# Start-up of a filter-and-mixer kernel: inputs of the first batch ahead of all else on two queues, more buffers for the token weights, second weights seven tiles ahead

## The chip, the cores and the metric

One core of one Trainium2 chip. The metric is the time of one execution in device microseconds (us), as the median of a kernel's runs. All runs told of here are of the fast state, at a granted TensorE clock of 0.988 to 0.995. Each ratio below is the mean time of one kernel's fast runs over that of the other's fast runs of the same rounds, so it is not quite the ratio of the medians that are quoted.

## The reference

A global filter along the sequence (transform, product with a complex filter, transform back), then an MLP mixer over tokens and over channels. Batch 8, sequence 3008, width 256, token width 256, channel width 1536.

```python
X = np.fft.rfft(x, axis=1)
Y = X * (filt_r + 1j * filt_i)[None]
x = np.fft.irfft(Y, n=3008, axis=1).astype(np.float32)
xt = x.transpose(0, 2, 1)
h = np.maximum(xt @ w_tok1, 0.0) @ w_tok2
u = x + h.transpose(0, 2, 1)
h2 = np.maximum(u @ w_ch1, 0.0) @ w_ch2
out = u + h2
```

All weights come as 64-bit floats and have to be converted on the chip.

## The kernel before

The start-up runs the filter of batch 0 alone, with nothing of the mixer to hide behind. Its x is multiplied by a first table (`wa0`), copied by ScalarE (ACT), turned by 16 VectorE (DVE) transposes, and then goes through 32 filter steps. A step takes a table `wb` (one load per two steps) and a piece of the filter `filt` (some loads per two steps), and its result is stored to memory as `g_tmp`, to be read back by token (`t4_load`). The token weights are loaded as raw words `st` and converted among the steps: one ACT and four DVE instructions, then either two TensorE (PE) additions and an ACT copy (`on_chip`) or one more DVE addition (`rounded`). One conversion goes through `begin` (issue its load), `copy` (first ACT instruction) and `end`.

```python
BY_PE = 6        # second token weights that PE adds up; the rest are rounded on DVE
EARLY = 12
# raw words of the weights, in buffers borrowed from later stages
early = [(up, "u")] * 2 + [(tp, "t")] * 2 + [(vp, "v")] * 2
late = [(t2p, "t2"), (t3p, "t3")]
stages = [(t4p, "t4")] * (A // 2) + early * 3 + late * 5      # A // 2 = 12

def filt_load(c, first):                    # first batch: everything on Pool's queue
    q = nc.gpsimd if first else nc.sync
    ...
def convert():                              # one tile: finish, start the next two's steps
    ended[0] += 1
    ...
    advance(end); advance(copy); advance(begin)

def x_load(b, c):                           # two loads a piece, all on SyncE
    where, tag = ((xp, "x"), (tp, "t"), (vp, "v"))[c % 3] if b == 0 else (xp, "x")
    ...
def w_load(c):                              # one table and one set of filter loads
    wbs[g] = wbp.tile([P, WC, P + KR], FP32, tag="wb", name="wb")
    nc.sync.dma_start(wbs[g], ...)
    filt_load(c, first)
...
# the driver: i < NXC (12) are the x steps, then 33 filter steps
    if i < NXC:
        if i in (0, 2, 4, 6): advance(begin)
        if i == 5: advance(copy)
        if i in (7, 9, 11): convert()
    else:
        if (i - NXC) % 3 == 2: convert()
        k = i - NXC - 2
        if 19 <= k < 25: t4_load(0, k - 19, 0, PARTS[1])   # read g_tmp back, on SyncE
        elif k == 25: next(second)                         # x of the next batch, on SyncE
        elif k in (30, 31): ...                            # more of g_tmp
...
for i in range(rounds, A // 2 + TC * N2 // NG):
    convert()
    ...
    if i == A // 2 + BY_PE - 1:
        sum_up()
        acc = token_sums(0)
h1s[0] = token_relu(acc)
```

Every store of `g_tmp` is issued by ACT.

Of the kernel before, what the change touches and what calls it, by code (L numbers as in the profile page):

```python
# [20 lines left out]
N2 = 64  # L21
# [3 lines left out]
K2 = 32  # L25
A = 24
KR = 4 * A
HALF = 64
XC = 2
NXC = A // XC  # L30
TC4 = 4
FB = 3
XB = 2
KC = 2
WC = 2
DT = 256
TC = DT // P
# [6 lines left out]
MT = 6  # L44
NG = 8
PARTS = (0, 64, 112)
BY_PE = 6
EARLY = 12
GROUPS = ((0,), (1, 2), (3, 4), (5, 6), (7,))


# [73 lines left out]
def kernel(  # L125
# [11 lines left out]
    nc = tc.nc  # L137
# [70 lines left out]
    def filt_load(c, first):  # L208
        t, k0 = filts[c % FB], c * KC

        q = nc.gpsimd if first else nc.sync
        for src, i, p0 in ((filt_r, 0, 0), (filt_i, 1, HALF)) + (() if first else ((filt_r, 0, HALF),)):
            q.dma_start(t[p0:p0 + A, i], raw(src, k0, [[64 * D, A], [D, KC], [1, D]]))
            lo = p0 + 32
            if k0 == 0:
                q.dma_start(t[lo:lo + A, i, 0, :], raw(src, 32, [[64 * D, A], [1, D]]))
            k = max(k0, 1)

            for j0, n in ((0, 16), (16, A - 1 - 16)):
                q.dma_start(t[lo + j0:lo + j0 + n, i, k - k0:KC, :],  # L220
                            raw(src, 64 * (j0 + 1) - k, [[64 * D, n], [-D, k0 + KC - k], [1, D]]))

    def filt_double(c):
# [2 lines left out]



    early = [(up, "u")] * 2 + [(tp, "t")] * 2 + [(vp, "v")] * 2
    late = [(t2p, "t2"), (t3p, "t3")]  # L230
    stages = [(t4p, "t4")] * (A // 2) + early * 3 + late * 5

    def stage(n):
        where, tag = stages.pop(0)
# [56 lines left out]
    def w1_load(i):  # L291
        st = stage(512)
        rows = moe_w_tok1.rearrange("(n2 n1) t -> n2 n1 t", n1=N1)
        q = nc.sync if i < EARLY else nc.gpsimd
        last = 2 * i + 2 == A
        if last:
            nc.gpsimd.memset(st.bitcast(U32)[HALF:P, 512:1024], 0)
        for h in range(2):
            n = 1 if last and h else 2
            lo = h * A + 2 * i  # L300
            q.dma_start(st[h * HALF:(h + 1) * HALF, 0:n * DT].rearrange("p (a t) -> p a t", t=DT),
                        rows[:, lo:lo + n, :])
        yield

        h = halves(st, 512, spare_pair())
        yield next(h)
        on_chip(wai_t, *next(h), 512, [(lambda v: v, w1[:, 2 * i:2 * i + 2, :].rearrange("p a t -> p (a t)"))])

    def w2_load(i):

        t, g = divmod(i, N2 // NG)
        n = NG * N1

        more = g + 1 < N2 // NG
        st = stage(512)
        nc.gpsimd.dma_start(st[:, 0:n + more], moe_w_tok2[ts(t, P), ds(g * n, n + more)])
        yield
        dst = w2[:, t].rearrange("p (a h n2) -> p h n2 a", h=2, n2=HALF)[:, :, ds(g * NG, NG), :]

        def some(h, nh, w):  # L320
            return (lambda v: bass.AP(tensor=v.tensor, offset=v.offset + h * A, ap=[v.ap[0], [A, nh], [N1, NG], [1, w]]),
                    dst[:, h:h + nh, :, 0:w])

        parts = [some(0, 2, A)] if more else [some(0, 1, A), some(1, 1, A - 1)]
        if i < BY_PE:
            h = halves(st, n + more, spare_pair())
            yield next(h)
            on_chip(ident, *next(h), n + more, parts)
        else:
            yield from rounded(st, n + more, parts, False)  # L330
# [44 lines left out]
    def advance(it):  # L375
        s = next(it, None)
        if s:
            next(s, None)

    def sum_up():  # L380
        while behind:
            behind.pop(0)[1]()

    def convert():

        ended[0] += 1
        while behind and behind[0][0] < ended[0] - 2:
            behind.pop(0)[1]()
        advance(end)
        advance(copy)  # L390
        advance(begin)



# [2 lines left out]
    def x_load(b, c):  # L397
        last = c == NXC - 1

        where, tag = ((xp, "x"), (tp, "t"), (vp, "v"))[c % 3] if b == 0 else (xp, "x")  # L400
        t = where.tile([P, XC, D], FP32, tag=tag, name="x")
        rows = x[b].rearrange("(n2 n1) d -> n2 n1 d", n1=N1)
        for h in range(2):
            n = XC - 1 if last and h else XC
            lo = h * A + c * XC
            nc.sync.dma_start(t[h * HALF:(h + 1) * HALF, 0:n, :], rows[:, lo:lo + n, :])
            if n < XC:

                nc.sync.dma_start(t[h * HALF:(h + 1) * HALF, n:XC, :], rows[:, lo:lo + 1, :])
        xs[b, c] = t  # L410

    def rows_of(t_d, b):
# [12 lines left out]
    def dft(bs):  # L425
# [9 lines left out]
                nc.sync.dma_start(wbs[g], (wbi0_d if first else wbi_d)[:, ts(g, WC), :])  # L435
            filt_load(c, first)

        ahead = 3 * XB if first else XB
        for u in todo[0:ahead]:
            x_load(*u)  # L440
        if not first:
            yield True
        for i, u in enumerate(todo):
            if first and i in (5, 8):
                w_load(i // 6)
            a_unit(*u)
            if i + ahead < len(todo):
                x_load(*todo[i + ahead])
            yield i + 1 < len(todo)
# [65 lines left out]
        for k in range(K2 + 1):  # L515
            if k < K2:
                b_unit(k)
                if k % KC == 0 and k // KC + 2 < K2 // KC:
                    t2_load(k // KC + 2)
                    w_load(k // KC + 2)  # L520
                if first and k % KC == KC - 1 and k + 1 < K2:
                    filt_double(k // KC + 1)
            if k >= 1:
                bi_unit(k - 1)
            yield
# [18 lines left out]
    def token_relu(acc):  # L544
        h1 = h1p.tile([P, TC, D], FP32, tag="h1", name="h1")
        nc.scalar.activation(out=h1, in_=acc, func=AF.Relu)
        return h1
# [219 lines left out]
    with tc.manual_schedule():  # L767
        nc.sync.dma_start(wa0, wa0_d)
        nc.vector.memset(turned[:, A:K2, :], 0.0)
        for t in filts:  # L770
            nc.vector.memset(t, 0.0)
        rounds = 0
        second = dft(GROUPS[1])
        for i, _ in enumerate(dft(GROUPS[0])):
            if i == 0:
                for t, src in ((wai_t, wait_d), (wa, wa_d), (wai, wai_d), (ident, ident_d)):
                    nc.scalar.dma_start(t, src)

            if i < NXC:
                if i in (0, 2, 4, 6):  # L780
                    advance(begin)
                if i == 5:
                    advance(copy)
                if i in (7, 9, 11):
                    convert()
                    rounds += 1
            else:
                if (i - NXC) % 3 == 2:
                    convert()
                    rounds += 1  # L790

                k = i - NXC - 2
                if 19 <= k < 25:
                    t4_load(0, k - 19, 0, PARTS[1])
                elif k == 25:
                    next(second)
                elif k in (30, 31):
                    for c in range(3):
                        t4_load(0, 3 * (k - 30) + c, PARTS[1], PARTS[2])
        for c in range(A // TC4):  # L800
            t4_load(0, c, PARTS[2], P)
        sum_up()
        both = wcp.tile([P, 2, JP, 7, P], FP32, tag="wc", name="wc")

        chan.extend((both[:, 0], both[:, 1]))
        for i in range(rounds, A // 2 + TC * N2 // NG):
            convert()
            if i - rounds < XB:
                next(second)
            if i == A // 2 + BY_PE - 1:  # L810
                sum_up()
                acc = token_sums(0)
        h1s[0] = token_relu(acc)
        for dh in range(DH):
            convert()
            u_part(0, 0, dh)
        for f in v_steps(0, 0):
            f()
        for _ in range(XB):
            next(second)  # L820
        group, todo, done = -1, iter(()), True

        def next_ready(b):
            return done or b != GROUPS[group][-1]

        for b, i, place in mix(next_ready):
            if group + 1 < len(GROUPS) and b == GROUPS[group + 1][0]:
                if not done:
                    raise AssertionError("the filter's steps don't fit beside the mixer's")
                group += 1  # L830
                done = group + 1 == len(GROUPS)
                todo = iter(()) if done else dft(GROUPS[group + 1]) if group else second
                spread = True

            if not done and (place == 1 or group == 0 and (spread and (place == 2 or i > 3) or place == 2 and i % 2)):
                spread = next(todo, "end")
                done = spread == "end"
# [30 lines left out]
```

## Time and profile before

2588.3 us in the median of three runs (2585.92 to 2592.76). The start-up falls into stages, whose joints stand in the timeline; what is left after the last conversion is the mixer.

| stage | from, to | before (us) |
|---|---|---|
| A | start to the first transpose | 31.14 |
| B | first transpose to the end of the last filter product | 91.01 |
| C | to the first sum `v` | 44.25 |
| D | to the end of the last channel-weight conversion | 56.22 |
| rest | to the end | 2364.6 |

B is 18.38 us (16 transposes and a hand-over, the same in every kernel below) and 72.63 us of filter steps; below, "B" is the second part alone.

### The profile page before, as it was taken

What the parts mean: (1) busy time and instruction counts of PE and PEld (TensorE: products, weight loads), DVE (VectorE), ACT (ScalarE), POOL (GpSimd) and SP (SyncE); (2) the same over time, 40 slices, a digit from 0 to 9 for tenths busy, and PEclk for the clock granted to TensorE, in tenths of its full rate; (3) what the DMA queues carried; (4) which work ended last, traced back from release to release, by engine and by line L of the source; (5) the groups of instructions that cost most, each with busy time, mean ns of one, the idle gap of its engine ahead of it and who ended that gap; (6) DMA issues with size and microseconds to landing.
All of it is one profiled execution on the core that took longest, in us unless ns stands there. A gap on an engine that the chain in (4) does not pass through costs nothing.

```text
span 2587.2 us, 31459 instructions
## 1 busy us (share of the span) xinstructions
PE 2505.6 (97%) x10952; PEld 2000.9 (77%) x10952; DVE 1816.0 (70%) x3458; ACT 691.2 (27%) x1347; POOL 526.9 (20%) x966
## 2 busy tenths in 40 slices
PE   5989999999999999999999999999999999999998
PEld 2556666788878777888787777788888888888887
DVE  6897888556675888746666788846678577647676
ACT  2433222123221222222321222212222122212222
POOL 3652211111211112112112111121121121211212
PEclk7999999999999999999999999999999999999999
DMA  6964333312232332202232233211232121100001
GB/s 167 232 195 155 109 106 103 106 48 90 90 90 64 88 88 71 80 17 89 90 96 77 75 84 87 80 31 57 90 85 75 50 64 53 25 9 8 17 12 21
DMA packets 151834, 205.20 MB, mean 79 GB/s; under 512 B 34216, under 2 KB 102034, under 8 KB 151676
## 3 DMA queue, kind: packets, MB, share of 16 engines
q1 hardware_dynamic: 81068, 115.65, 15.7%
q0 software_dynamic: 30656, 39.93, 6.4%
q10 hardware_dynamic: 39952, 47.61, 5.7%
q8 instruction: 87, 1.43, 0.2%
q14 instruction: 71, 0.58, 0.1%
HBM read 131.23 MB, written 71.83 MB: 78 GB/s over the span
## 4 chain that ended last, share of the span: by engine, by line
PE 78%; DVE 13%; issue 3%; DMA 3%; ACT 2%; SPq 0%; ACTq 0%; POOL 0%; DVEq 0%; POOLq 0%
PE ps_po L631 26%; PE ps_pg L597 15%; PE ps_pg L613 11%; PE ps_b L540 4%; PE ps_b L557 4%; DVE t L575 3%; DVE hh L575 3%; PE ps_acc L540 2%; PE ps_acc L557 2%; PE ps_acc L494 2%; PE ps_b L562 2%; PE ps_acc L417 2%; DVE u L575 2%; DVE s L575 1%; PE ps_b L470 1%
## 5 line engine op out<-in xcount | busy, mean ns | idle before, releaser
L575 DVE TENSOR_TENSOR hh<-ps_pg,s 128x512 f32<-128x512 f32 (+3 forms) x864 | 482.4, 586 | 624.4 <-ACT s L600 623.8
L676 POOL DMA_DIRECT2D out_dram<-r x757 | 409.8, 550 | 1949.1 <-ACT hh L618 929.0
L618 ACT ACTIVATE hh<-hh 128x512 f32<-128x512 f32 (+1 forms) x576 | 348.0, 621 | 1122.8 <-DVE hh L575 1122.8
L631 PE MATMUL ps_po<-t,wc 128*128 128x256 f32 (+1 forms) x2304 | 535.5, 375 | 5.4 <-DVE t L575 4.6
L631 PEld LDWEIGHTS ps_po<-t,wc 128*128 128x128 f32 x2304 | 434.5, 190 | 132.9 <-issue 53.3
L631 PE MATMUL ps_po<-hh,wc 128*128 128x256 f32 (+1 forms) x1728 | 413.2, 375 | 3.1 <-POOL wc L339 2.8
L597 PE MATMUL ps_pg<-v,wc 128*128 128x256 f32 (+1 forms) x1728 | 413.3, 375 | 0.2
L631 PEld LDWEIGHTS ps_po<-hh,wc 128*128 128x128 f32 x1728 | 327.5, 190 | 42.4 <-POOL wc L339 3.6
L597 PEld LDWEIGHTS ps_pg<-v,wc 128*128 128x128 f32 x1728 | 326.9, 190 | 40.5 <-DVE v L575 3.0
L613 PE MATMUL ps_pg<-u,wc 128*128 128x256 f32 (+1 forms) x1152 | 294.5, 378 | 7.0 <-DVE hh L575 6.5
L575 DVE TENSOR_TENSOR t<-t,hh 128x256 f32<-128x256 f32 (+1 forms) x576 | 242.0, 420 | 19.8
L613 PEld LDWEIGHTS ps_pg<-u,wc 128*128 128x128 f32 x1152 | 216.2, 190 | 43.5 <-DVE hh L575 17.4
L575 DVE TENSOR_TENSOR s<-ps_pg,hh 128x512 f32<-128x512 f32 (+1 forms) x288 | 196.0, 681 | 30.7 <-DVE hh L575 0.9
L575 DVE TENSOR_TENSOR t<-hh 128x512 f32<-128x512 f32 (+1 forms) x288 | 192.7, 669 | 0.6 <-ACT hh L618 0.6
L597 PE MATMUL ps_pg<-u,wc 128*128 128x256 f32 (+1 forms) x576 | 169.9, 377 | 1.6 <-DVE hh L575 1.6
L613 PE MATMUL ps_pg<-v,wc 128*128 128x256 f32 (+1 forms) x576 | 169.2, 375 | 0.0
L600 ACT COPY s<-ps_pg 128x256 f32<-128x256 f32 (+1 forms) x288 | 106.0, 368 | 154.7 <-PE ps_pg L597 151.5
L613 PEld LDWEIGHTS ps_pg<-v,wc 128*128 128x128 f32 x576 | 108.9, 190 | 13.3
L597 PEld LDWEIGHTS ps_pg<-u,wc 128*128 128x128 f32 x576 | 102.7, 191 | 20.3 <-issue 8.8
L540 PE MATMUL ps_b<-t,w 128*128 128x256 f32 x480 | 106.3, 384 | 4.3 <-DMA t<-g_tmp 4.3
L557 PE MATMUL ps_b<-w,h 128*128 128x512 f32 (+1 forms) x232 | 107.8, 587 | 0.0
L540 PEld LDWEIGHTS ps_b<-t,w 128*128 128x128 f32 x480 | 92.2, 192 | 17.9 <-issue 4.0
(102 smaller groups left out, 2251.4 us busy)
## 6 DMA issues: line engine op xcount, KB each, us to landing
g_tmp<-t ACTq DMA_DIRECT2D x128, 192.0 KB
x<-in_x_dram SPq DMA_DIRECT2D x184, 128.0 KB
out_dram<-r POOLq DMA_DIRECT2D x698, 32.0 KB, 1.8
z_tmp<-t ACTq DMA_DIRECT2D x84, 256.0 KB
t<-z_tmp SPq DMA_DIRECT2D x112, 192.0 KB
t<-g_tmp SPq DMA_DIRECT2D x42, 512.0 KB
wb<-wbi_t SPq DMA_DIRECT2D x80, 224.0 KB
filt<-in_filt_r_dram SPq DMA_DIRECT2D x128, 48.0 KB
```

The source lines that it names most:

```text
L417: nc.tensor.matmul(ps, wa0 if b == 0 else wa, xs.pop((b, c)).rearrange("p a d -> p (a d)"), start=True, stop=True)
L494: nc.tensor.matmul(ps[0:KR], wbs[k // WC][:, k % WC, P:], p, start=(i == 0), stop=(i == len(parts) - 1))
L540: nc.tensor.matmul(acc[:, t, :], w1[:, a, ts(t, P)], t4[b, a // TC4][:, a % TC4, :], start=(a == 0 and t == 0), stop=(a == A - 1 and t == ...
L557: nc.tensor.matmul(ps[:, 0:w], h1[:, t, ts(dh, P)], w2[:, t, ds(m * 512, w)], start=(t == 0), stop=False)
L562: nc.tensor.matmul(ps[:, ds(q * P, n)], t4[b, c][:, r, ts(dh, P)], wai[:, 0:n], start=False, stop=(q == 3))
L575: nc.vector.tensor_tensor(out=out, in0=in0, in1=in1, op=op)
L597: nc.tensor.matmul(ps[:, 0:hw], chan[0][:, jp, n, :], mov, start=True, stop=True)
L600: nc.scalar.copy(out=s[:, 0], in_=g[0][:, 0, 0:hw])
L613: nc.tensor.matmul(ps[:, 0:hw], chan[0][:, jp, n, :], mov, start=True, stop=True)
L618: nc.scalar.activation(out=hs, in_=hs, func=AF.Relu)
L631: nc.tensor.matmul(po[i][:, j, 0:hw], chan[1][:, jp, n, :], mov, start=(jp == 0 and first == 1), stop=(jp == JP - 1 and last == 1))
L676: q.dma_start(rows[g, e, :, ds(h * A + 4 * m, n)], blocks[ts(g, CW), h, e, 0:n])
```

## The change

Intent: begin the turning earlier by bringing x in first, from SyncE and Pool at once, in twelve buffers of its own; fill the time of the turning, in which DMA idled, with the twelve first token weights, each in a buffer of its own; load second weights up to seven tiles ahead, and let PE add up more of them. Some filter pieces of the first batch move from Pool's queue to SyncE's, since Pool now also has half of x.

```diff
-BY_PE = 6
-EARLY = 12
+BY_PE = 8
+BY_PE_LAST = 3
+BESIDE = 13
 # filt_load: the last pieces, from the fourth set on, to SyncE
-                q.dma_start(t[lo + j0:lo + j0 + n, i, k - k0:KC, :],
+                (nc.sync if first and j0 and c >= FB else q).dma_start(t[lo + j0:lo + j0 + n, i, k - k0:KC, :],
 # buffers of the raw weights
-    early = [(up, "u")] * 2 + [(tp, "t")] * 2 + [(vp, "v")] * 2
-    late = [(t2p, "t2"), (t3p, "t3")]
-    stages = [(t4p, "t4")] * (A // 2) + early * 3 + late * 5
+    round_ = [(p_, t_) for p_, t_ in ((up, "u"), (tp, "t"), (vp, "v"), (t2p, "t2")) for _ in range(2)]
+    stages = [(t4p, "t4")] * 7 + round_ * 3 + [(t2p, "t2"), (t3p, "t3")] * 5
 # w1_load, w2_load
-        q = nc.sync if i < EARLY else nc.gpsimd
+        q = nc.sync
-        if i < BY_PE:
+        if i < BY_PE or i >= TC * N2 // NG - BY_PE_LAST:
 # convert: up to seven tiles ahead (four near the end)
-        advance(begin)
+        while begun[0] < len(tiles) and begun[0] < ended[0] + (4 if begun[0] >= len(tiles) - len(LAST) else 7):
+            start()
 # x_load of the first batch: buffers of its own, second half on Pool
-        where, tag = ((xp, "x"), (tp, "t"), (vp, "v"))[c % 3] if b == 0 else (xp, "x")
+        where, tag = ((xp, "x"), (t1p, "t1"), *round_[0::2])[c // 2] if b == 0 else (xp, "x")
+            q = nc.gpsimd if b == 0 and h else nc.sync
-        ahead = 3 * XB if first else XB
+        ahead = NXC if first else XB
-            if first and i in (5, 8):
-                w_load(i // 6)
+            if first and i < FB:
+                w_load(i)
 # the driver: token loads from x step 3 on, two a step up to step 8
-                if i in (0, 2, 4, 6):
-                    advance(begin)
-                if i in (7, 9, 11):
+                if i >= FB:
+                    for _ in range(2 if i < 9 else 1):
+                        start()
 # conversions beside the filter steps: 13, spread evenly
-                if (i - NXC) % 3 == 2:
+                if k >= 0 and (k + 1) * BESIDE // (K2 + 1) > k * BESIDE // (K2 + 1):
                     convert()
 # after the token sums, ahead of the relu
+        sum_up()
         h1s[0] = token_relu(acc)
```

(The lines that begin with # are added here.)

More of the change, by code (lines that the diff above doesn't have):

```diff
@@ L378, in advance, with start @@
             next(s, None)
+    begun = [0]
+    def start():
+        advance(begin)
+        begun[0] += 1
     def sum_up():
@@ L405, in x_load @@
             lo = h * A + c * XC
-            nc.sync.dma_start(t[h * HALF:(h + 1) * HALF, 0:n, :], rows[:, lo:lo + n, :])
+            q = nc.gpsimd if b == 0 and h else nc.sync
+            q.dma_start(t[h * HALF:(h + 1) * HALF, 0:n, :], rows[:, lo:lo + n, :])
             if n < XC:
-                nc.sync.dma_start(t[h * HALF:(h + 1) * HALF, n:XC, :], rows[:, lo:lo + 1, :])
+                q.dma_start(t[h * HALF:(h + 1) * HALF, n:XC, :], rows[:, lo:lo + 1, :])
         xs[b, c] = t
@@ L517, in dft @@
                 b_unit(k)
-                if k % KC == 0 and k // KC + 2 < K2 // KC:
+                if k % KC == 0 and k // KC + 2 < K2 // KC and (k or not first):
                     t2_load(k // KC + 2)
@@ L771 @@
             nc.vector.memset(t, 0.0)
-        rounds = 0
         second = dft(GROUPS[1])
@@ L779 @@
             if i < NXC:
-                if i in (0, 2, 4, 6):
-                    advance(begin)
-                if i == 5:
+                if i >= FB:
+                    for _ in range(2 if i < 9 else 1):
+                        start()
+                if i == NXC - 1:
                     advance(copy)
-                if i in (7, 9, 11):
+            else:
+                k = i - NXC - 2
+                if k >= 0 and (k + 1) * BESIDE // (K2 + 1) > k * BESIDE // (K2 + 1):
                     convert()
-                    rounds += 1
-            else:
-                if (i - NXC) % 3 == 2:
-                    convert()
-                    rounds += 1
-                k = i - NXC - 2
                 if 19 <= k < 25:
@@ L805 @@
         chan.extend((both[:, 0], both[:, 1]))
-        for i in range(rounds, A // 2 + TC * N2 // NG):
+        for i in range(BESIDE, A // 2 + TC * N2 // NG):
             convert()
-            if i - rounds < XB:
+            if i - BESIDE < XB:
                 next(second)
```

## The prediction

> **What bounds the kernel now.** I read the page's slices first, then the busy time in 20 us windows, then the chain that ended last for the first 330 us, then the timeline around each joint of that chain.
>
> The page says that the whole kernel is a TensorE (PE) kernel: PE is busy 97% of the span, at nine tenths in every slice but the first two. The change touches only what happens before that, so the question is how many us of the start-up can go.
>
> ```profile
> span 2587.2 us, 31459 instructions
> PE 2505.6 (97%) x10952; PEld 2000.9 (77%) x10952; DVE 1816.0 (70%) x3458; ACT 691.2 (27%) x1347; POOL 526.9 (20%) x966
> PE   5989999999999999999999999999999999999998
> ```
>
> The windows show what limits the start (busy us of PE, weight loads, DVE, ACT, POOL; then granted clock, DMA share, GB/s):
>
> ```profile
> 0.00:20.00 20.00, 9.51 (x15) 3.22 (x16) 5.86 (x7) 5.83 (x9) 11.06 (x24) 0.95 0.82 213
> 20.00:40.00 20.00, 10.29 (x14) 3.40 (x12) 14.22 (x19) 5.93 (x10) 0.00 (x0) 0.67 1.00 234
> 40.00:60.00 20.00, 11.17 (x33) 6.55 (x34) 17.44 (x28) 4.18 (x9) 5.77 (x11) 0.69 0.18 49
> 60.00:80.00 20.00, 19.26 (x71) 11.50 (x69) 18.14 (x41) 10.31 (x21) 14.27 (x27) 1.00 0.84 222
> 100.00:120.00 20.00, 16.71 (x58) 9.40 (x59) 15.73 (x37) 7.38 (x16) 9.95 (x18) 1.00 1.01 261
> 120.00:140.00 20.00, 16.07 (x48) 8.93 (x47) 15.78 (x36) 11.03 (x20) 3.90 (x7) 0.94 1.01 237
> ```
>
> Up to 31 us DMA is the limit; from 40 to 60 us DMA idles (0.18) while VectorE (DVE) turns the data; from 60 to 100 us DVE and PE are both nearly full; from 100 to 140 us DMA is full and both wait. The chain and the timeline name the joints:
>
> ```profile
> 8.20 5.17 DMA x<-in_x_dram
> 16.11 5.83 DMA st<-in_moe_w_tok_dram
> 23.15 5.15 DMA x<-in_x_dram
> 102.90 7.12 DMA filt<-in_filt_r_dram
> 110.31 6.07 DMA filt<-in_filt_r_dram
> 132.29 4.50 DMA t<-g_tmp
> 136.93 22.66 PE ps_b L540 x96
> ```
>
> ```profile
> 31.14 17.00 DVE L455 STREAM_TRANSPOSE turned<-turned 128x512 f32<-128x512 f32 x16 [1.87 <-ACT turned L419]
> 49.52 0.42 DVE L482 TENSOR_TENSOR p<-ps_b,filt 128x256 f32<-128x256 f32 x1 [1.39 <-issue]
> 121.73 0.42 DVE L484 TENSOR_TENSOR p<-ps_pg,filt 64x256 f32<-64x256 f32 x1
> 136.93 22.64 PE L540 MATMUL ps_b<-t,w 128*128 128x256 f32 x96 [3.40 <-DMA t<-g_tmp]
> ```
>
> So there are four stages. A, until the turning starts at 31.14: x comes in, with token weights (st) and filters between. B, from the turning to the end of the first batch's filter at 122.15 (121.73 + 0.42): the turning, then 32 filter steps with 11 weight conversions among them. C, to the v sums at 166.40: the first token sums wait for g_tmp until 136.93, take 22.7 us, then the relu and u. D, to about 222: the channel weights are converted on DVE beside the first mixer steps. After that the kernel is a full PE pipeline that only shifts.
>
> **What the Trainium skill says.** "DMA: Bandwidth & Descriptors", section "Issuing engines are not separate DMA queues": DMAs of all issuers run on the same 16 engines, and issuing from several saves only issuing time. The trace agrees: share 0.82 in the first window with two issuers, 1.00 in the second, 213 and 234 GB/s. So splitting x over SyncE and Pool helps by order and issue, not by bandwidth. The same page, "Queues, rings and completion order": an engine goes round-robin between queues, and a queue is consumed in ring order. So x first on both queues goes ahead of all else, and a load issued behind eight 256 KB weight loads waits for them; before, st in the middle of x did just that at 16.11. "TensorE: Matmul & The Clock Gate", "What's actually happening": an idle PE falls to half clock. The trace agrees: the x matmuls take 2.05 us after waits and 1.02 to 1.12 in a dense run, with a granted clock of 0.67 in the second window. A denser x phase should therefore keep pace.
>
> **The change part by part.**
>
> Stage A. x is 3.1 MB. Before, SyncE alone issues its 25 pieces at some 0.64 us apiece, with three token tiles (512 KB each) before the last piece, and filters on Pool ahead of most of it. After, the order of instructions has 12 x pieces on SyncE and 13 on Pool as the first of each, at 0.55 to 0.6 us an issue, so both are issued after about 8 us and bandwidth rules. Bytes ahead of the last x: 3.15 MB, 0.32 MB of tables, and about 0.3 MB that slips in from the faster queue, 3.8 MB. In steady flow the first 20 us moved about 250 GB/s, from a start near 2 us: 15 us, landing at 17. One matmul (about 1.1 us) and its ACT copy (0.6) with their hand-overs put the turning at some 19.1 us in place of 31.14. **A: -12.0 us.** Three token conversions (4 DVE instructions, 2.26 us each) that sat in DVE's idle time of this stage move into later work.
>
> Stage B. The turning is unchanged (17.0 us) and the 1.4 us to the first product too. Then 32 steps of three DVE instructions: 1.34 us each without a wait (60.08, 61.42, 62.76), 42.9 us. Before, 11 conversions ran among them, 9 of 512 columns at 2.26 and 2 of 377 at 1.85: 24.0 us; sum 66.9, measured 72.6 from 49.52 to 122.15, so 5.7 us of waits. After, BESIDE is 13, and the order puts 12 full ones before the last product: 27.1, sum 70.0. PE is level with this: a step is 1.56 us there (61.04, 62.60) and a conversion 1.72, so 32 x 1.56 + 11 x 1.72 = 68.8; the two interlock not quite perfectly, so 71.5. Waits after: all 12 token tiles and three second ones now load from about 17 us on, into the time in which DMA idled: 3.5 + 1.2 (filters, first tables) + 6.2 + 1.1 = 12 MB at 250 GB/s, done near 50 us. The fourth table and filter pieces queue behind the last 2 MB of it and land at about the time that step 6 wants them (50 us): 1 us lost. Late in the stage five second weights (1.9 MB) still compete with filters, g_tmp and x, so DMA is near full again, but the Pool issues 4 filter pieces per pair of steps rather than 6, and no token tiles are left: 1 us lost. Total 73.5. **B: +1.0 us.** Its end is then near 111 in place of 122.15.
>
> Stage C. Before, the token sums start 14.8 us after B's end, and the wait is g_tmp's. After, eight PE-added tiles stand ahead of them in PE's order: 8 x 1.85 of DVE = 14.8, plus PE's last pair 1.3 and hand-overs: 16.5. **+1.7.** BY_PE_LAST puts three more tiles' PE additions behind the token sums and ahead of the relu, because everything left is summed up there: a tile costs 1.27 us of PE (123.06 to 124.32), 3.8 together, and its ACT copy of 0.8 stands ahead of the relu in ACT's order. **+4.7.** What this buys, five fewer DVE roundings (0.66 us net each, 3.3 us), lies beside the 22.7 us of token sums, where DVE has room: from B's end 14.8 + 5 x 2.61 + 3 x 1.85 = 33.4 us, before the sums end at 39.1. It buys nothing there. **C: +6.4.**
>
> Stage D: the same ten conversions, 11 to 12 us per mixer step as before; **0**. The main part only shifts.
>
> Sum: -12.0 + 1.0 + 6.4 = -4.6; 2588.3 - 4.6 = **2583** us, rounded down because the B waits are my most guarded term.
>
> **The rivals.**
>
> R1: the gain stays. If B runs without waits (71.5) and the token sums start with g_tmp no later than before, the sum is -12 - 1 + 4.7, or -8; and if ACT and PE find the three late tiles already hidden, -13: 2575. For it: DMA's idle window of 40 to 60 us is worth 0.8 x 20 = 16 us of transfer, and the 100 to 120 us waits come from that backlog. Against it: the order of instructions really has the three additions ahead of the relu.
>
> R2: DMA takes it back. By B's end some 25 MB must have moved; at 245 GB/s that is 102 us plus 2, near the 111 that I allow. If the small filter rows keep the rate at 222 GB/s, as between 60 and 80 us, it is 115, and with second weights prefetched seven tiles ahead in front of the filters on Pool's queue 3 to 5 us more are lost: 2587 to 2589.
>
> R3: the start is worse. Pool's issue now puts the first filters behind 13 x pieces, and the turning could be followed by a wait for filter or table. The turning ends near 36 us and the filters should land by 25, so there are 10 us to spare; I give it little weight. It would make 2590.
>
> R4: the change reaches the mixer, through clock or buffers. Nothing in the order of instructions there differs, so only noise (2586 to 2593 in three runs) speaks for it.
>
> **Range and chances.** Two per cent is 52 us; the whole start-up to 166 us has no such sum to give, and no part adds that much. So "same" is nearly certain: faster 0.01, same 0.98, slower 0.01. The 8-in-10 range spans R1 to R2 with run noise: 2572 to 2590.
>
> **What would show it.** Right: the turning starts at 18 to 21 us; DMA share over 0.8 from 20 to 50 us; the last filter product at 108 to 114; token sums 15 to 18 us after it; about 5.5 us from their end to the relu's, against 0.6 now; the same 56 us from v to the last conversion. Wrong: a start of turning after 24 us (Pool's queue is slow with x), DMA waits on filt or wb of over 6 us in B, token sums that still wait for g_tmp, or a mixer part whose length differs by more than 3 us.

## More of the kernel before

The prediction shows the page, the windows and the chain of this profile. Three lines more, from its timeline (columns: start, duration, engine, line, what, how many, and in brackets the idle time ahead and what ended it; SPq is SyncE's sequencer): the last table is issued at 108.19, the relu starts as soon as the token sums end, and `v` 6.8 us after that.

```profile
108.19 0.33 SPq L435 DMA_DIRECT2D wb<-wbi_t  x1
159.61 0.60 ACT L546 ACTIVATE h<-ps_b 128x512 f32<-128x512 f32 x1 [5.34 <-PE ps_b L540]
166.40 0.92 DVE L575 TENSOR_TENSOR v<-u 128x512 f32<-128x512 f32 x1 [1.75 <-ACT u L564]
```

## The result, and the profile after

2602.64 us in the median of four runs (2599.29 to 2603.0), beside 2587.61 of the kernel before in the same rounds (2585.92 to 2592.76): ratio 1.0052, 95% interval 1.0034 to 1.0069. It is slower by some 14 us where 5 us faster had been predicted, and outside the range of 2572 to 2590; within 2%, as its chance of 0.98 for "same" had said.

The page of the changed kernel, its span and PE's slices: 14.0 us more, and the first three slices, which were 5, 9 and 8, are now 4, 8 and 9.

```profile
span 2601.2 us, 31514 instructions
PE   4899999999999999999999999999999999999997
```

The stages, with the term of the prediction beside each:

| stage | before | after | difference | predicted |
|---|---|---|---|---|
| A | 31.14 | 19.67 | -11.5 | -12.0 |
| B (steps alone) | 72.63 | 88.73 | +16.1 | +1.0 |
| C | 44.25 | 51.02 | +6.8 | +6.4 |
| D | 56.22 | 57.42 | +1.2 | 0 |
| rest | 2364.6 | 2366.0 | +1.4 | 0 |

So one term is far off. The windows of the changed kernel (busy us of PE, weight loads, DVE, ACT, Pool; granted clock, DMA share, GB/s) show where. From 20 to 40 us DMA is full and DVE turns the data, as was hoped. From 40 to 60 us PE works 9.84 us and DVE 11.30, though the turning is over at 37: both wait, and DMA, at 0.74 and 182 GB/s, isn't full all the time either: its share is 0.48 from 46 to 50 us, 1.02 from 50 to 55 and 0.44 from 55 to 60. From 100 to 120 us it is the same again, with DMA nearly full.

```profile
20.00:40.00 20.00, 3.24 (x8) 2.02 (x9) 18.50 (x21) 1.82 (x3) 4.73 (x9) 0.53 1.04 253
40.00:60.00 20.00, 9.84 (x31) 5.69 (x30) 11.30 (x25) 4.34 (x9) 6.39 (x12) 0.76 0.74 182
100.00:120.00 20.00, 12.43 (x45) 7.00 (x43) 12.67 (x28) 7.18 (x15) 5.79 (x11) 0.92 0.95 233
```

The timeline of the changed kernel names the two waits, and the joints of stage C:

```profile
15.98 35.90 SPq L302 DMA_DIRECT2D st<-in_moe_w_tok_dram  x24
19.67 16.99 DVE L465 STREAM_TRANSPOSE turned<-turned 128x512 f32<-128x512 f32 x16 [13.45 <-ACT turned L429]
51.98 0.53 SPq L445 DMA_DIRECT2D wb<-wbi_t  x1
57.48 1.22 PE L480 MATMUL ps_b<-turned,wb 128*128 128x256 f32 x2 [8.76 <-DMA wb<-wbi_t]
58.80 0.42 DVE L492 TENSOR_TENSOR p<-ps_b,filt 128x256 f32<-128x256 f32 x1 [7.31 <-PE ps_b L480]
106.33 8.43 SPq L416 DMA_DIRECT2D x<-in_x_dram  x4
121.19 0.42 DVE L492 TENSOR_TENSOR p<-ps_b,filt 128x256 f32<-128x256 f32 x1 [7.44 <-PE ps_b L480]
145.65 20.88 PE L550 MATMUL ps_b<-t,w 128*128 128x256 f32 x96
170.97 0.63 ACT L556 ACTIVATE h<-ps_b 128x512 f32<-128x512 f32 x1
177.80 0.69 DVE L585 TENSOR_TENSOR v<-u 128x512 f32<-128x512 f32 x1 [2.53 <-ACT u L574]
```

The twenty-four loads of the token weights (`st`) keep SyncE's sequencer for 35.90 us. The fourth table stands behind them, is issued at 51.98 and lets PE go on at 57.48, after 8.76 us. Later four loads of the next batch's x keep the same sequencer for 8.43 us (3.06 before), and the last table behind them comes late by some 7 us again. The two waits of DVE add up to 14.75 us. (Of the 16.1 us of B, 3.0 are work, DVE being busy for 66.62 us in place of 63.57, and 13.1 are idle time, 22.11 us in place of 9.06.)

Why does the sequencer take so long? Its own waits, from 14 to 60 us and in the chain from 102 us on (columns of the first: us in total, times, longest; between the two, ACT's issue of the store that the longest waits for):

```profile
SPq L302 <- DMA st<-in_moe_w_tok_dram: 13.9, 11, 3.0
SPq L302 <- DMA g_tmp<-t: 8.5, 2, 6.6
```

```profile
42.94 0.33 ACTq L515 DMA_DIRECT2D g_tmp<-t  x1
```

```profile
102.41 10.54 DMA g_tmp<-t
114.86 4.97 DMA wb<-wbi_t
```

While it issues loads that need nothing of `g_tmp`, the sequencer waits for earlier loads to land, and for stores of `g_tmp` that ACT issues. The longest of these waits lasts from 40.48 to 47.07 us, for a store that ACT issued only at 42.94: in the program as built, the load that is held shares its semaphore with that store. From 106 us on a load of x is held in the same way for 6.1 us. A store of 192 KB took 10.54 us from issue to completion when DMA was full, the issue of x waited for it, and the table waited for the issue of x.

### The profile page after: what moved, and what is told of

It is laid out like the page before. It is cut to its first block, busy times and chain, and to the rows that moved or that the text cites. A ratio compares the mean times of both kernels' runs of the same rounds, so it can differ in the third digit from the quotient of the medians.

```text
span 2601.2 us, 31514 instructions
## 1 busy us (share of the span) xinstructions
PE 2513.9 (97%) x10972; PEld 2007.3 (77%) x10972; DVE 1810.9 (70%) x3451; ACT 694.7 (27%) x1354; POOL 519.2 (20%) x953
## 4 chain that ended last, share of the span: by engine, by line
PE 79%; DVE 11%; issue 2%; DMA 2%; ACT 2%; POOL 1%; ACTq 0%; DVEq 0%; SPq 0%; POOLq 0%
PE ps_po L641 27%; PE ps_pg L607 16%; PE ps_pg L623 12%; PE ps_b L550 4%; PE ps_b L567 4%; PE ps_acc L550 2%; DVE t L585 2%; PE ps_acc L567 2%; DVE hh L585 2%; PE ps_b L572 2%; PE ps_acc L504 2%; PE ps_acc L427 2%; PE ps_b L504 1%; PE ps_b L480 1%; PE ps_acc L480 1%
## 5 line engine op out<-in xcount | busy, mean ns | idle before, releaser
L504 PE MATMUL ps_acc<-p,wb 128*96 128x256 f32 (+1 forms) x256 | 97.0, 481 | 8.1 <-DVE p L496 3.7
```

Source lines behind the costliest of these rows:

```text
L504: nc.tensor.matmul(ps[0:KR], wbs[k // WC][:, k % WC, P:], p, start=(i == 0), stop=(i == len(parts) - 1))
```

## The experiments

Three theories for stage B. **T1, order:** two blocks of loads stand ahead of tables in SyncE's in-order queue, and the tables wait for the issue of the blocks, not for bandwidth. **T2, bytes:** the change moves so much into the first 120 us that the engines of DMA are simply full; whatever the order, something waits. **T3, foreign completions:** filter pieces and other loads on SyncE's queue take turns with ACT's stores of `g_tmp` on the same completion semaphores, so SyncE's issues wait for stores. Each run below is read by the same joints (us; "waits" are DVE's idle times over 1 us in the filter steps; "sums" is from B's end to the first token sum, "relu" from the last sum to the relu).

| kernel | A | B | DVE's waits in B | sums | relu | C | D | span |
|---|---|---|---|---|---|---|---|---|
| before | 31.14 | 72.6 | 1.73 | 14.78 | 0.04 | 44.25 | 56.22 | 2587.2 |
| changed | 19.67 | 88.7 | 7.31, 1.50, 7.44 | 18.87 | 4.44 | 51.02 | 57.42 | 2601.2 |
| filt_pool | 20.39 | 82.6 | 8.05, 1.05, 1.84 | 18.52 | 4.43 | 50.67 | 56.56 | 2594.7 |
| x_later | 20.02 | 85.5 | 6.93, 1.60, 2.83, 1.64 | 28.06 | 4.44 | 60.21 | 56.63 | 2607.3 |
| few_start | 20.26 | 81.4 | 2.67, 2.01, 2.81, 2.13 | 18.86 | 4.43 | 51.00 | 56.20 | 2593.9 |
| x_only | 29.40 | 72.4 | 1.33, 1.24 | 15.39 | 0.04 | 45.06 | 55.56 | 2586.1 |
| tab_pool | 19.42 | 79.9 | 1.10, 2.10, 2.44 | 18.52 | 4.44 | 50.67 | 56.54 | 2591.2 |
| few_filt | 20.10 | 75.0 | 2.16, 1.08 | 18.87 | 4.44 | 51.02 | 56.42 | 2585.7 |
| pe_before | 19.95 | 87.5 | 8.08, 1.62, 4.67, 1.01 | 15.21 | 0.04 | 47.62 | 57.99 | 2598.3 |
| best1 | 20.43 | 74.0 | 1.18 | 15.23 | 0.04 | 47.69 | 55.36 | 2579.9 |
| g_pool | 19.86 | 84.5 | 4.66, 1.75, 3.22, 2.98 | 18.91 | 4.44 | 51.06 | 59.90 | 2599.9 |
| best2 | 20.48 | 73.7 | 1.24 | 18.87 | 0.04 | 46.58 | 55.41 | 2580.5 |
| best3 | 20.74 | 73.1 | 1.42 | 14.86 | 4.60 | 47.16 | 55.25 | 2579.9 |

The rest lies between 2364.0 and 2366.8 in every one of them. All results were correct.

### filt_pool: filter pieces of the first batch all on Pool's queue again

```diff
-                (nc.sync if first and j0 and c >= FB else q).dma_start(t[...
+                q.dma_start(t[...
```

> The changed kernel with the third filter pieces of the first batch back on Pool's queue; nothing else. Theories for stage B, which took 88.7 us in the changed kernel against 72.6 before. T1 (order): two blocks in SyncE's in-order queue, the 24 token loads ahead of the fourth table (DVE waits 7.3 us at 51 to 59) and the second batch's x loads ahead of the last table (7.4 us at 114 to 121). T2 (bytes): the DMA engines are simply full, and a wait that is taken away comes back elsewhere. T3 (filter pieces): the two pieces per table in SyncE's queue make loads there wait for the g_tmp stores. Expected: T1 and T2: first wait still 7 us, second still over 4 us, total 2599 to 2604. T3: the second wait goes, total near 2595.

2597.77 us (2596.84 to 2598.24), ratio to before 1.0036 [1.0021, 1.0051]. The late wait of 7.44 falls to 1.84, the early one stays at 8.05; B is 6.1 us shorter. The filter pieces on SyncE cost one of the two waits. T3 had forecast this; T1 and T2 had both put the late wait at over 4 us. The total lies between T3's 2595 and the 2599 of the others. The four loads of x go out in 3.45 us in place of 8.43: with fewer loads in the joint order, the eighth DMA before each of them is an older one, and none is a store that is still under way.

### x_later: x of the next batch issued after the last loads of g_tmp

```diff
-                elif k == 25:
-                    next(second)
...
         for c in range(A // TC4):
             t4_load(0, c, PARTS[2], P)
+        next(second)
```

> The changed kernel with the first x loads of the second batches (four pieces, 0.5 MB) moved in SyncE's order from ahead of the last table to behind the last g_tmp loads; nothing else. T1: the wait of 7.4 us for the last table goes, nothing comes back, stage B takes about 81 us, total near 2595. T2: the wait shrinks by the 0.5 MB alone, 2 us, or is moved to the g_tmp loads ahead of the token sums: total 2600 to 2603.

2608.11 us (2606.68 to 2609.15), ratio 1.0076 [1.0061, 1.0091]. The wait of 7.44 for a table does go, to 2.83 and 1.64. T1 had expected that, but also that nothing comes back; the 2.83 us are for a filter piece that SyncE could issue only after 6.0 us of waiting for a store of `g_tmp`, which fits T3. Both forecasts of the total (near 2595, or 2600 to 2603) missed: the run is slower, and not a clean test, since the products of this x stand ahead of the token sums in PE's order, and now they wait for x instead.

```profile
136.52 2.04 PE L427 MATMUL ps_b<-x,wa 128*128 128x512 f32 x2 [6.82 <-DMA x<-in_x_dram]
```

### few_start: one token load a step from the start

```diff
-                    for _ in range(2 if i < 9 else 1):
+                    for _ in range(1):
```

> The changed kernel with nine weight tiles begun in the prologue rather than fifteen; the other three first token weights and the second ones are begun from the conversions on. T1: the fourth table is no longer behind all 24 token loads, the wait of 7.3 us near 50 us falls under 2 us, total near 2595. T2: the 2.6 MB that are put off come back as waits of the same size later in stage B, total 2600 to 2604.

2595.06 us (2592.49 to 2597.26), ratio 1.0026 [1.0011, 1.0041]. Three tiles fewer stand ahead of the fourth table, and the early wait is gone, with the total that T1 had forecast (near 2595). What remains are four waits of 2.0 to 2.8 us after 102 us, 9.62 us together beside the one of 7.44 before; this run puts bytes off as well, so it does not tell order from bytes there.

### x_only: the kernel before with only the new loading of x

```diff
-        where, tag = ((xp, "x"), (tp, "t"), (vp, "v"))[c % 3] if b == 0 else (xp, "x")
+        where, tag = ((xp, "x"), (t1p, "t1"), (up, "u"), (tp, "t"), (vp, "v"), (t2p, "t2"))[c // 2] if b == 0 else (xp, "x")
...
-            nc.sync.dma_start(t[h * HALF:...
+            q = nc.gpsimd if b == 0 and h else nc.sync
+            q.dma_start(t[h * HALF:...
-        ahead = 3 * XB if first else XB
+        ahead = NXC if first else XB
```

> The kernel before with one part of the change alone: the x pieces of the first batch as the first of SyncE's and Pool's queues, in twelve buffers; weights, filters, conversions and their order as before. T1: the turning starts near 19.7 us as in the changed kernel, stage B stays near 73 us, all after it is as before, total 2576 to 2580. T2: the DMA waits that the kernel before has from 100 to 117 us grow by what was gained: stage B near 82 us, total 2585 to 2589.

2587.41 us (2585.99 to 2587.88), ratio 0.9995 [0.9978, 1.0011]: the same as before. This is the total that T2 had forecast (2585 to 2589), but not by its cause, since B did not grow (72.4): T1's condition, a turning from 19.7 us on, was not met. The turning starts at 29.40, only 1.7 us earlier. Here the first conversions are still among the x steps, and their ACT instruction, which waits for its weights, stands in front of the copies that the turning needs:

```profile
20.25 0.66 ACT L245 ACTIVATE both<-st 128x512 f32<-128x512 f32 x1 [6.82 <-DMA st<-in_moe_w_tok_dram]
```

So the gain of A is not from the order of x alone. By this line it needs the conversions moved out of the stage, which the change does as well; moving them alone was not tried.

### tab_pool: as filt_pool, and the tables from the fourth on issued by Pool

```diff
-                nc.sync.dma_start(wbs[g], ...
+                (nc.gpsimd if first and c >= FB else nc.sync).dma_start(wbs[g], ...
```

> The changed kernel with the tables from the fourth on and the filters' third pieces on Pool's queue; no byte more or less, the token loads, x loads and g_tmp loads on SyncE as they were. This moves only the order. T1 (order): both waits for a table (7.3 and 7.4 us on DVE) fall under 2 us, stage B takes 74 to 77 us, and the total is near 2588 to 2591. T2 (bytes): tables still come late because the engines are full until 46 us and from 100 us on: stage B over 82 us, total over 2595.

2593.97 us (2593.35 to 2595.56), ratio 1.0027 [1.0010, 1.0043]. The token loads keep SyncE's sequencer for 39.94 us here, four us longer than in the changed kernel, yet no product waits for a table near 59 or 121 us, since the tables no longer stand behind them. The same bytes flow, and the window from 40 to 60 us now moves 232 GB/s in place of 182:

```profile
15.03 39.94 SPq L302 DMA_DIRECT2D st<-in_moe_w_tok_dram  x24
42.76 0.54 POOL L445 DMA_DIRECT2D wb<-wbi_t  x1 [14.63 <-DVE p L494]
40.00:60.00 20.00, 15.79 (x56) 8.98 (x55) 17.51 (x39) 8.19 (x17) 14.24 (x27) 0.95 0.87 232
```

This decides against T2 for the early wait: nothing was taken off DMA, and the 7.31 us are gone. It does not tell waiting to be issued from standing behind bytes in SyncE's queue, because on Pool's queue, issued at 42.76, the table is free of both (see g_pool). Two smaller waits for filter pieces, which now stand behind tables in Pool's order, come at 84 to 91 us (1.10, 2.10), and one for PE at 97 us (2.44). With them B (79.9) and the total lie between what T1 (74 to 77; 2588 to 2591) and T2 (over 82; over 2595) had forecast.

### few_filt: filt_pool and few_start together

> The changed kernel with both measures that helped alone: nine tiles begun in the prologue (stage B 81.4 us alone) and the filters' third pieces back on Pool (82.6 us alone), against 88.7. T1: the two waits are separate, so the gains add: stage B near 75.5 us, total near 2589. T2: what is put off meets the full stretch after 100 us, stage B stays over 80 us, total 2594 or more.

2587.25 us (2586.59 to 2588.38), ratio 0.9999 [0.9984, 1.0014]. B is 75.0 us: 13.7 less than in the changed kernel, where the two edits alone gave 6.1 and 7.4. They add up, as T1 had forecast (75.5, total near 2589), which fits two separate waits. The timeline shows the token loads issued in about half the time, and the fourth table early:

```profile
16.33 18.45 SPq L302 DMA_DIRECT2D st<-in_moe_w_tok_dram  x18
43.39 7.66 SPq L445 DMA_DIRECT2D wb<-wbi_t  x3
```

### pe_before: additions by PE as in the kernel before

```diff
-BY_PE = 8
-BY_PE_LAST = 3
+BY_PE = 6
+BY_PE_LAST = 0
```

> The changed kernel with BY_PE back at 6 and BY_PE_LAST at 0: as many tiles added by PE as before, none between the token sums and the relu. Stage C took 51.0 us from the end of the filter to the v sums, 44.25 before; the relu began 4.4 us after the token sums' end rather than at once. By the prediction's working of stage C: the relu at once (-4.4), the token sums 2 to 4 us earlier, stage C 44 to 47 us, total 2595 to 2598. If the late tiles hide something else, C stays over 49 us and the total over 2600.

2600.72 us (2600.46 to 2602.6), ratio 1.0052 [1.0037, 1.0067]. C falls from 51.02 to 47.62, that is by 3.4 and not by the 6.4 that the prediction charges to these two numbers. The token sums begin 3.7 us sooner and the relu 4.4, but then 11.5 us pass from the relu to `v` in place of 6.8: PE waits for a rounding of DVE. The forecast (C 44 to 47, total 2595 to 2598) missed.

```profile
166.52 1.75 PE L567 MATMUL ps_acc<-w,h 128*128 128x512 f32 x2 [2.77 <-DVE w L274]
173.47 0.69 DVE L585 TENSOR_TENSOR v<-u 128x512 f32<-128x512 f32 x1 [1.13 <-ACT u L574]
```

### best1: few_filt and pe_before, and the last weights' two buffers in the other order

```diff
-    stages = ... + [(t2p, "t2"), (t3p, "t3")] * 5
+    stages = ... + [(t3p, "t3"), (t2p, "t2")] * 5
```

> All of it together: nine tiles begun in the prologue, filters' third pieces on Pool, BY_PE 6 and BY_PE_LAST 0, and the last ten stages starting with the other buffer (so that the second late weight does not wait for a buffer that is still read). T1: turning near 20 us, stage B near 75.5, stage C near 46, stage D near 56.2: v at 160.5, total 2581 to 2584, faster than before by 5 us or more. T2: stage B over 80 us, total 2587 or more.

2582.98 us (2581.86 to 2583.64), ratio 0.9982 [0.9967, 0.9996]: as forecast (2581 to 2584), faster than the changed kernel, and than the kernel before by 0.2%, with an interval that only just leaves out 1. The order of the buffers is for stage D. In the changed kernel Pool's issue of the last weights stood still for 21.80 us, until a conversion had freed its buffer, where before it was issued some 30 us sooner (first line after, second before):

```profile
175.08 3.88 POOL L346 DMA_DIRECT2D st<-in_moe_w_ch_dram  x8 [21.80 <-DVE both L253]
```

```profile
145.40 2.04 POOL L345 DMA_DIRECT2D st<-in_moe_w_ch_dram  x4 [2.02 <-issue]
```

D is 55.36 in best1, 56.42 in few_filt and 57.42 in the changed kernel. The order alone was not tried, so the 1.1 us between the first two are not proved to be its.

### g_pool: stores of g_tmp of the first batch from Pool

```diff
-                    nc.scalar.dma_start(g_d[b, ts(c, KC)]...
+                    (nc.gpsimd if first else nc.scalar).dma_start(g_d[b, ts(c, KC)]...
```

> The changed kernel with one thing moved: the stores of g_tmp of the first batch go out from Pool instead of ScalarE; loads and their order on SyncE stay. Theory T3 (SyncE's issues wait for completions of g_tmp stores; 8.5 of the 22.4 us of its waits in the first 60 us named a g_tmp store): the second wait for a table, near 121 us, falls from 7.4 to under 2 us; the first, near 59 us, shrinks from 7.3 to some 3 or 4 us but stays, since the waits for token weights remain; first product to last product 78 to 81 us instead of 88.7; total 2592 to 2596. Theory T1 alone (a plain backlog in SyncE's order, whoever stores): both waits stay within 1.5 us of 7.3 and 7.4, first to last product over 86 us, total 2599 or more.

2601.15 us (2596.43 to 2602.68), ratio 1.004 [1.0025, 1.0055]. The early half came as T3 said: SyncE's issues of `st` name no store of `g_tmp` any more (8.5 us before), their block shrinks from 35.90 to 29.07 us, and the early wait from 7.31 to 4.66. The 6.8 us that the block lost are nearly the 8.5. But the table gained little by it: issued at 45.10, 6.9 us sooner than in the changed kernel, it let PE go on at 55.05, only 2.4 us sooner. It was under way for 9.95 us in place of 5.50, with DMA full (1.02 from 46 to 50 us, 0.94 from 50 to 55), so on SyncE's queue the bytes of the block ahead of it still held it up.

```profile
15.37 29.07 SPq L302 DMA_DIRECT2D st<-in_moe_w_tok_dram  x24
45.10 0.33 SPq L445 DMA_DIRECT2D wb<-wbi_t  x1
55.05 1.22 PE L480 MATMUL ps_b<-turned,wb 128*128 128x256 f32 x2 [6.12 <-DMA wb<-wbi_t]
```

The late half missed. The x loads went out in 3.37 us in place of 8.43, but the wait went elsewhere: the chain now has a filter piece on SyncE that took 7.22 us to land, and DVE waited 3.22 and 2.98 us.

```profile
106.72 7.22 DMA filt<-in_filt_r_dram
```

There, DMA is full (0.90 from 100 to 120 us), and D is 59.90 with Pool's queue longer. Here T1's total was nearer (it expected 2599 or more), and T3's 2592 to 2596 was wrong.

### best2 and best3: two further splits of the additions

Both with the edits of few_filt and the other order of the buffers; best2 has BY_PE = 8 and BY_PE_LAST = 0, best3 has 6 and 2.

> The changed kernel with filter pieces on Pool, one token tile a step from the start, no late token tiles (0 for 3), the eight early tiles by TensorE kept, and the last two parts of token weights in swapped order. Theory: first to last product near 74 us; token sums begin some 15.2 us after it as without late tiles or 18.5 if the late tiles are not what delayed them; relu at once after the sums; the two paths into v (TensorE's and VectorE's roundings) nearly in balance, so relu start to last channel sum adds up to C near 46 us; total 2581 to 2582.5, 1 us under the version with six early tiles (2583.0). Rival: VectorE bounds v all the same and C stays at 47.5 or over, total 2583 or over.

> As the run before it, but with six early tiles by TensorE and two late ones instead of eight and none. Theory: two late tiles put some 3 us of additions ahead of relu and take some 5 us from VectorE after it; C near 46.5 us, first to last product near 74 us, total 2581 to 2583. Rival: the late tiles cost what they save, C 48 or more, total 2583.5 or more.

best2: 2582.36 us (2581.05 to 2582.95), ratio 0.997 [0.9953, 0.9986]. best3: 2583.53 us (2582.0 to 2587.48), ratio 0.9977 [0.9963, 0.9992]. In best2 the relu follows the sums at once and `v` comes 6.8 us after it, as in the kernel before; C is 46.58, near the 46 expected, and the total is as forecast (2581 to 2582.5). best3 lies at the edge of its rival (2583.5 or more), through one run of 2587.48, with C at 47.16, between the 46.5 and the 48 of the two. The rival's cost shows in part: two late tiles put the relu 4.60 us late, as three had, since DVE, with more roundings ahead, delivers the last of their halves only 1.2 and 3.0 us after the end of the sums.

```profile
131.46 20.88 PE L550 MATMUL ps_b<-t,w 128*128 128x256 f32 x96
152.38 0.60 ACT L556 ACTIVATE h<-ps_b 128x512 f32<-128x512 f32 x1 [5.13 <-PE ps_b L550]
159.17 0.69 DVE L585 TENSOR_TENSOR v<-u 128x512 f32<-128x512 f32 x1 [1.55 <-ACT u L574]
```

The three intervals overlap, so no one of them is shown to be the best; each beats the kernel before by 0.2 to 0.3% and the changed one by some 20 us.

## Why the prediction was wrong

**Stage A was right in size, in part by luck.** -12.0 predicted, -11.5 measured (19.67). Its working names the order of x; x_only shows that this by itself is worth 1.7 us, and its trace points to the three conversions moved out of the stage, which the prediction only mentions as work that moves later, as what lets it count. Nor were both halves of x "issued after about 8 us": SyncE's twelve loads took it until 14.36 us, 6.2 of them waiting for landings, the same mistake as in B, here without a cost that shows. And the 250 GB/s of the first 20 us, counted from 2 us on, are 235 in the trace.

**Stage B is the step that failed:** "The fourth table and filter pieces queue behind the last 2 MB of it and land at about the time that step 6 wants them (50 us): 1 us lost." The place was right and the reckoning was not. It divided bytes by a bandwidth: 12 MB at 250 GB/s, done near 50 us. The bytes did come at about this rate (253 GB/s from 20 to 40 us), but a table behind them in SyncE's queue has two waits to pass. It is issued only after the twenty-four loads ahead of it, and for 22.4 us of those 35.9 the sequencer waited, for landings of its own loads and of ACT's stores. Then it lands behind what the queue still holds. So the table was issued at 51.98 and let PE go on at 57.48: 7.31 us lost on DVE in place of 1. tab_pool takes the table out of this queue and few_start shortens the block: either removes the wait. g_pool takes away the waits for stores: 2.65 us of the 7.31 go, and 4.66 stay.

The second sentence of the step, "no token tiles are left: 1 us lost", missed a wait of 7.44 in the same manner. The prediction counted filter pieces per queue ("the Pool issues 4 filter pieces per pair of steps rather than 6") and took this as relief for Pool; it didn't ask what the two pieces that went to SyncE do to the loads of x and the last table there. filt_pool takes 6.1 us off B by undoing that. With both undone, B is 75.0, beside 73.5 predicted: the working for conversions and steps held.

That it is the place in SyncE's queue and not the sum of bytes is shown for the early wait (tab_pool); how it divides between late issue and bytes ahead in the queue rests on g_pool alone. For the late one, DMA is at 0.95, and both may have a part: x_later and filt_pool reduce it by order alone, but g_pool and few_start leave or bring waits of 2 to 3 us there, so some of it is likely a full DMA. How much, stays open.

**Rival R2** ("DMA takes it back", 2587 to 2589) had the right stage and the right sign, at a third of the size, but it put the loss on filters behind second weights in Pool's queue, where it came on SyncE's, and it too counted only bytes. R3, a wait right after the turning, did not come: the first product follows it after 1.39 us, as before. "DMA waits on filt or wb of over 6 us in B" was listed as what would show it wrong, and both came.

**Stage C was right in size and wrong in one claim.** +6.8 measured, +6.4 predicted: the late additions put the relu 4.4 us behind the sums (4.7 predicted). The token sums began 4.1 us later after B's end in place of 1.7, and were 1.8 us shorter (20.88 us for 22.64), which cancels most of it: that the sum fits so well is luck. "It buys nothing there" failed: undoing it all gives back 3.4 us of 6.8, because with fewer additions on PE, DVE's roundings reach past the token sums and hold up `v` (pe_before). Keeping eight early tiles and no late one gives 46.58, 1.1 us below pe_before's way (47.69 in best1).

**Stage D** was predicted at 0 and is +1.2, with Pool's wait for a buffer as the likely cause (not tried alone). **The rest** only shifts, as predicted (2364.6 and 2366.0), well within the 3 us that R4 needed.

## What to carry to other kernels

Before adding loads to a queue, list in order what stands behind them on the issuing engine, and ask when the last of them is *issued* as well as when their bytes are through; a load behind them passes both waits. Small loads that the very next step needs belong ahead of the block or on another issuer's queue. A queue that shares completion semaphores with another engine's stores inherits their delays, so a load moved to an idle-looking queue is not free. And when a gain of 11 us at the start turns into a loss, first line up the joints of both traces: four subtractions named the stage here.

## What the Trainium skill lacked or had wrong

- "DMA: Bandwidth & Descriptors", section "Issuing engines are not separate DMA queues": it says that issuing from several engines only saves time on the sequencer, "which is usually small relative to the DMA itself". Here it was not small: the twenty-four loads took SyncE's sequencer 35.90 us, 13.5 of them issuing and 22.4 waiting for earlier DMAs, and with the same bytes and only other issuers for tables and filter pieces (tab_pool) the kernel ran in 2593.97 us in place of 2602.64, as a load on another issuer's queue also gets past the bytes of the block.
- Same page, section "Anatomy of one DMA — SWDGE (gpsimd) path": it says that DMA engines don't wait on semaphores and that any wait happens on the issuing sequencer before dispatch, which fits all that is seen here. What it lacks is the consequence for order: waits of SyncE's issues for landings of earlier loads (13.9 us in 11 waits) and of another engine's stores (8.5 us in two), which held up a table that needed neither.
- Same section: its fit for one DMA that Pool issues, about 2.0 us plus the bytes over 436 GB/s, leaves out what else is queued. By it a filter piece of 48 KB would take 2.1 us, as an estimate from the page; Pool's pieces of 32 to 48 KB took 6.5 to 7.5 us in the median from 95 to 118 us, where DMA was nearly full. A store of 192 KB that ACT issued there took 10.54 us to completion; the page has no fit for that issuer.
- "TensorE: Matmul & The Clock Gate", section "What's actually happening": nothing wrong; it says that an idle PE runs at half clock, and after the wait of 8.76 us a pair of matmuls took 1.22 us, beside 0.59 in a dense run, at a granted clock of 0.50 from 55 to 60 us.
